# A linear-attention block followed by a three-way maxout layer: k and v laid out as five or four tokens per partition, projections in two-bank tiles, the maxima of q as a factor on the numerators, and a new order of the work

## The chip, the cores and the metric

One core of one Trainium2 chip. The time is device microseconds for one execution of the whole program. A core has TensorE (PE, with its weight loads PEld), VectorE (DVE), ScalarE (ACT), GpSimd (POOL) and SyncE (SP, here a queue for transfers), and 16 DMA engines that all queues share. [...]

## The reference

```
phi(x):  p = x @ w_phi                       # 64 -> 128 features
         p = p - max(|p|)                    # over the features, for each token
         concat(exp(p), exp(-p))             # 256 features
attention, for each of 8 batches x 8 heads, 576 tokens, 64 wide:
         kv = phi(k).T @ v ;  z = sum(phi(k))
         x  = (phi(q) @ kv) / (phi(q) @ z + 1e-6)
feed-forward, on 4608 tokens of 512 (the 8 heads side by side):
         h = max(x @ w1, x @ w2, x @ w3) ;  out = h @ w_out      # 512 -> 768 -> 512
```

Inputs and outputs are float32; products are made in bfloat16. Note that phi subtracts the maximum m *before* the sign is taken: the two halves are exp(p - m) and exp(-(p - m)), so m does not cancel between them.

## The kernel before, in words

**Units and chunks.** Attention is cut into 16 units (`attention`): four heads of one batch, two pairs of heads each. The feed-forward part is cut into nine chunks (`chunk`) of 512 tokens: one for each batch, for the first 512 tokens of it, and a last one for the 64 tokens left over in each of the 8 batches. A chunk needs both units of its batch.

**Layout.** A head's first 512 tokens lie four to a partition over 128 partitions; its last 64 tokens, the *tail*, lie one to a partition over 64 (L364-L376). So a unit has 18 tiles of 128 tokens: 16 main ones and two tail tiles, each made of the tails of two heads. One load brings a unit's main part, two more bring the tails of both units of a batch. For the first four units q and k are loaded by POOL with a cast to bfloat16 on the way (L472), apart from the first k, and turned on PE (L515, evicted at L518). From the fifth unit on they are loaded as float32 by SP, cast on POOL (L502), and turned by a DMA transpose, q and k side by side (L528).

**A unit, step by step.** *Projection* (L555): for each tile one product for q on the upper 64 rows and one for k on the lower 64 rows, each into a bank of its own for four tiles. *Exponentials of k*: `Ek`, both signs, from PSUM (L568). *Maxima*: DVE reduces the absolute values, `mk` and `mqp` (L574). *Factors of k*: `em` = exp(+-mk) is multiplied into v (`vab` L616, and `vtl` for the tails L631, both on POOL), so that Ek need not wait for the maxima. *Maxima of q*: in the first four units PE subtracts them with products of -1 (L655); from the fifth on PE turns the maxima (L582), ACT or DVE copies them out (L586), a DMA writes them as row 64 of `qkT` (L590), and a product with 65 rows (L651) gives p - m. *Exponentials of q*: `Eq`, from that product (L663). *K and N*: kv with z as a 65th column (L680, L683, evicted at L687), and the numerators with the denominator as a 65th column, both signs added in PSUM (L701). *Quotient*: reciprocal (L707) and product (L708) on DVE. *Turn of x*: on PE for the first six units (L721, evicted at L724), by a DMA transpose after that (L731).

**A chunk.** Two sets of six products `ups` (L754), with the weights w2 - w1 and w3 - w1; the first is evicted with a maximum against 0 (L762 on ACT, L764 on DVE), the second with a maximum against that (L760). Then for each of four tiles of 128 tokens a straight part x @ (w1 @ w_out) (L782) and the part of h (L787), evicted (L795) and stored (L802). The weights arrive by casting loads on POOL (L432); their differences are made on POOL and DVE (L829); w1 @ w_out is made on PE (L841, L855, L859).

**What sets the order.** A table in the source, `PLAN`, made by a planner, names for each node its engine, its start in the plan and the PSUM bank or buffer that it takes. `plan` reads it, `fill` puts small idle products on PE into gaps of the first 28 us. The engines are in-order queues; the framework puts the waits. `GATES` (L483) holds back some early loads of v until q and k of an earlier unit are turned.

Of the kernel before, what the change touches and what calls it, by code (L numbers as in the profile page):

```python
# [19 lines left out]
P = 128  # L20
CT = DM // P
JT = DFF // P

SM = 512
ST = S - SM
HU = 4
UNITS = B * H // HU
UT = 18
MT = 16
GROUPS = [(0, 4), (4, 4), (8, 4), (12, 4), (16, 2)]  # L30
BATCHES = [(0, 8), (8, 8), (16, 2)]
EW = UT * P + D
XW = SM + P
BY_PE = 4
X_PE = 6
SUBT = 4
HALVES = 1
WARM = 28.0
SLOW = 4.6
JOIN = 2  # L40
MOVE = 5
VA_DVE = 1
QK = 3
OSB = 4
K0_SP = 1
GATES = (None, (0, 0), (1, 0), (2, 0))
V_ACT = 4

class Buf:


    def __init__(self, pool, make):
        self.pool, self.make = pool, make
        self.users, self.tile, self.index, self.left, self.free = [], None, None, 0, 0.0
        self.locked = 0.0

    def __call__(self):
        if self.tile is None:
            self.tile = self.make(self)
        return self.tile  # L60


class Lock:
    locked = 0.0


class Slots:


    def __init__(self, n):  # L70
        self.last = [None] * n


class Node:


    def __init__(self, kind, u, costs, fn, deps, bufs, locks=(), lat=0.0, pipe=0.0, hold=None, dmas=1,
                 packet=60.0, mode=0):
        self.kind, self.u = kind, u
        self.costs, self.fn, self.deps = costs, fn, list(deps)  # L80
        self.bufs, self.locks, self.lat, self.pipe = list(bufs), list(locks), lat, pipe
        self.hold, self.dmas, self.packet, self.mode = hold, dmas, packet, mode
        self.start = self.end = self.eng = None
        for b in self.bufs:
            b.users.append(self)

PLAN = """  # L90
9S0@0.4 6G0@0.4 2D0@0.4 3D@0.8 4S@1.0 7G@1.2 0G@2.1 11S@2.2 1G@2.8 8S0@2.8 91G1@3.3 10A@3.5 13S@4.1 90G@4.2 5D@4.4
18T1@4.4 170G2@5.0 19D0@5.1 12A@5.3 15S0@5.3 168G@5.8 24T002300@5.9 92D@5.9 29T45@6.1 27D@6.4 25A@6.4 20T6@6.4
1143G@6.7 30A@6.8 28D@7.0 16G@7.5 21D@7.6 26A@7.8 17G@7.8 95G@8.1 32D@8.2 22T7@8.2 31A@8.2 94G@8.3 34T12@8.4 244G0@8.6
169S0@8.7 100T6@8.8 23D@8.8 35A@8.9 39T34@9.0 37D@9.1 44T7@9.3 243G@9.4 41A@9.5 42D@9.7 36A@10.0 171S0@10.0 47D@10.3
1146G@10.3 40A@10.4 33D@10.6 62T10@10.8 45A@10.9 1144G@11.1 59T3@11.2 14S@11.2 38D@11.2 49A0@11.4 63A@11.6 68T5@11.6
101D1@11.8 1145G@11.9 43D@12.0 46A@12.1 98T2@12.2 69A@12.4 96T6@12.6 48D@12.6 60A@12.9 247G@12.9 99D@13.0
122T11411@13.2 175G@13.2 61A@13.6 97D@13.6 117T72@13.8 93S@13.9 70A@14.0 65T3@14.2 125D@14.2 53A@14.5 121D@14.6
176G@14.8 64A@14.8 248G@15.0 177T6@15.1 120D@15.2 57G0@15.2 118A@15.3 179T5@15.5 126D@15.8 66A@15.8 107T17@16.1
178D2@16.1 124A@16.3 58G@16.5 67A@16.6 111D@16.7 181T6@16.9 123A@17.1 180D@17.3 119A@17.5 102T34@17.6 109A@18.0
182D@18.0 112T25@18.1 110D@18.2 52A0@18.4 71T6@18.4 108A@18.6 55G@18.6 116D@18.8 388S0@18.9 253T1@18.9 103A@19.1  # L100
254D0@19.4 1153T7@19.5 131A1@19.6 54G@19.6 105D@19.6 72A@19.8 1155T1@20.1 114A@20.2 115D@20.2 50G@20.6 136A1@20.7
1157T3@20.7 106D@20.8 56A@20.9 113A@21.1 140T21@21.3 1154D0@21.4 104A@21.6 51G@21.6 76T50@21.7 73A@22.1 143T4@22.3
127A@22.4 1158D@22.6 135G@22.6 77A@22.7 74T6@22.8 1156A@23.1 149T7@23.4 82T50@23.6 316S0@23.7 75D@23.7 128G1@23.9
137T3@23.9 151A@24.0 83D0@24.2 78T1@24.4 150A@24.5 80T6@24.7 172D1@24.8 142A@24.9 132G@24.9 79D1@24.9 251T5@25.1
144A@25.3 249T7@25.6 81D0@25.6 130A@25.8 129G@25.9 134A@26.0 146T1@26.1 141A@26.1 250D@26.3 84T6@26.5 318S@26.6
139A@26.6 201T00200@26.9 245D@26.9 133G@26.9 252D@27.0 152T71@27.1 145A@27.1 138A@27.6 85D1@27.6 86T4@27.7 154T5@28.1
153A@28.1 87D@28.3 202A@28.5 315S@28.5 158T31@28.7 147A@28.8 205D@29.0 156T6@29.0 1159T7@29.3 203A@29.4 157D0@29.6
155A@29.8 148A@30.2 159D1@30.2 88T4@30.6 204D@30.8 1160A@30.9 192T5610@31.0 162T3@31.6 200D@31.7 194A@31.7 1163T2@31.9
317S@32.3 199D@32.4 198A@32.5 195D@33.0 193A@33.0 160T7@33.2 197A@33.5 164T1@33.5 163D0@33.6 1165T5@33.8 165A@34.1
161D1@34.2 1148G@34.2 1164A@34.7 89D@34.8 273T11011@35.1 196D@35.3 183T3172@35.5 276D@35.9 166T4@36.0 184A@36.2  # L110
1149G@36.3 1161T6@36.3 167D@36.6 1166A@36.7 186D@37.1 174S@37.1 189A@37.2 1175T4@37.6 185A@37.7 190D@37.7 188A@38.1
1162D@38.3 392G1@38.4 218T50@38.5 275A@38.6 1147G@38.6 1179T3@38.9 1176A1@39.0 277D@39.1 187D@39.5 219A@39.5
1177T7@39.8 173S@40.0 191D@40.1 220A@40.1 274A@40.6 1150D@40.7 255T6415@40.8 1178A@40.9 1151D@41.3 215T2@41.3
260A@41.5 1169T0@41.8 322G2@41.8 1180D@41.9 257A@42.0 217A@42.5 1152D@42.5 1173T3@42.7 393G@42.9 261A@43.0 262D@43.1
321G@43.2 1185T7@43.5 258D@43.7 1174A@43.8 387S@43.8 206A0@44.3 391G@44.3 259D@44.3 1171T1@44.4 216A@44.5 1170D@44.9
256A@45.1 1183T3@45.3 210G0@45.3 263D@45.5 1186D@46.1 1181T6@46.1 264T2045@47.1 1182D@47.3 320S0@47.5 212T7@47.7
269A@47.8 267D@47.9 1189T6@48.1 213A@48.4 207G0@48.5 1172D@48.5 265A@48.8 1191T2@49.0 246S@49.0 272D@49.1 266A@49.5
271D@49.7 323S1@49.7 1201T1@49.8 211A@50.0 270A@50.2 1190D@50.3 208G@50.4 224T4@50.7 1184D@50.9 221T5@50.9 226A@51.2
1187T6@51.4 268D@51.5 223A@51.6 214A@52.1 1192D@52.2 209G@52.2 296T31@52.2 1197T0@52.5 390G@52.5 225A@52.6 1188D@52.8
278A1@52.9 298A@53.2 287T7@53.3 281G1@53.5 297A@53.7 284T2@53.8 283G1@53.8 222A@54.0 229T40@54.2 279G@54.4 290T3@54.8  # L120
230A@55.1 227T5@55.3 285A@55.5 237T40@55.9 289A@56.0 1198T@56.2 282G@56.3 292A@56.5 460S0@57.0 291A@57.1 1202T@57.5
280G@57.5 288A@57.6 461S@57.6 1199D0@57.8 286A@58.1 228D@58.4 238D0@58.8 342T00600@58.8 389S@58.9 233T3@59.0
1203A1@59.1 231T7@59.4 346D@59.4 458S0@59.5 234D1@59.7 324T0254@59.8 343A@59.9 528S@60.1 293T1@60.3 344A@60.4
331D@60.5 326A@60.7 299T31@60.8 327D@61.1 459S@61.3 325A@61.3 301T5@61.4 232D0@61.7 294A@61.8 1205T0@62.0 300A@62.3
332D@62.3 302A@62.7 394S2@62.8 235T7@62.9 328D@62.9 295A@63.1 305T31@63.2 307T5@63.5 345D@63.5 329A@63.6 309T2@63.8
308D1@64.1 303T1@64.2 330A@64.2 1206T@64.5 236D0@64.7 304D1@65.3 239T6@65.8 310D0@66.0 1207A2@66.0 333T5471@66.2
532G0@66.5 306D1@66.6 533G@66.7 313T2@66.8 335A@66.9 464G2@67.0 241T0@67.1 340D@67.2 1193T3@67.4 339A@67.4 336D@67.8
240A@67.9 531G@68.1 311T7@68.3 314D@68.4 338A@68.5 1194T@68.6 337D@68.9 242A@69.0 319S@69.1 465G@69.1 312D@69.5
334A@69.7 527S@69.7 413T11511@69.9 341D@70.0 395T6207@70.2 414A@70.3 1195D3@70.6 350A0@70.7 347T4@70.7 1215T1@70.8
401A@71.0 398D@71.2 348A0@71.5 1211T3@71.7 400A@71.7 417D@71.8 349S@71.9 402D@72.1 397A@72.2 1219T4@72.5 466S0@72.6  # L130
1216A0@72.7 403D@72.7 351G0@72.9 1212A@73.2 399D@73.3 1209T6@73.4 1220A@73.7 416D@74.0 404T0173@74.4 415A@74.4
355A0@74.8 352G@74.8 362T40@74.9 1210A@75.0 407D@75.1 1213T5@75.2 406A@75.5 412D@75.7 1223T6@76.0 364A@76.0 411D@76.3
1214A@76.5 354G@76.7 1217T0@76.9 597S0@76.9 353A@77.0 1224D@77.2 396A@77.2 665S@77.5 410A@77.7 408D@77.8 359T7@77.8
530G@77.9 418T5@78.0 371T20@78.1 363A@78.2 1218D@78.4 421A1@78.6 373T6@78.7 361A@78.9 419D1@79.0 423G1@79.0 596S0@79.1
368T4@79.3 1221T0@79.4 374D@79.6 370A@79.7 409A@80.0 485T00500@80.3 420S@80.3 372A@80.5 1229T6@80.5 488D@80.8
595S@81.0 1222D@81.1 486A@81.3 356T3@81.4 369A@81.6 1227T2@81.6 1204S@81.6 489D@81.7 405A@81.9 668G1@82.0 1230D@82.1
598S@82.2 487A@82.4 1225T0@82.5 1228D@82.7 358A@82.8 422G@83.0 365T4@83.3 357A@83.4 1208S@83.5 1226D@83.6
476T1652@83.7 360A@83.9 664S@84.1 433T31@84.2 367A@84.4 479D@84.4 430T0@84.4 1231T7@84.7 482A@84.9 601G2@84.9
# [130 lines left out]
def fill(order, spare, make, ready):  # L269
# [649 lines left out]
```

## Time and profile before

| | us |
|---|---|
| runs of the kernel before | 298.52, 300.09, 303.92 (median 300.09) |
| span of the profiled execution, first to last instruction | 298.8 |
| PE busy | 284.6 (95%) |
| DVE busy | 209.1 (70%) |
| ACT busy | 200.4 (67%) |
| POOL busy | 137.6 (46%) |
| moved by DMA | 50.02 MB in 87879 packets |

The profiled execution is known by its span alone; it lies between the fastest and the median run. In a row of a *table of groups* stand line, engine, operation, out<-in, shapes, count, then busy us and mean ns of one, then the idle time before and what ended it. A row of the *timeline* has start, length, engine, line, operation, tensors and how many neighbours were merged (x6). A row of the *chain* has start, length and what was being done on the way that ended last. A busy PE is not PE at its peak, because matmuls overlap; the distance between starts is the better measure.

### The profile page before, as it was taken

To read this page: it belongs to the slowest core of one execution; us is meant where nothing else is said; L and a number is where in the kernel's file an instruction comes from. 1 tells how busy PE (TensorE), PEld (TensorE's weight loads), DVE (VectorE), ACT (ScalarE), POOL (GpSimd) and SP (SyncE) were. 2 spreads that over 40 slices of the span, in tenths; PEclk is the share of its full clock that TensorE was granted. 3 is DMA by queue.
4 is the path that set the end of the run, shared out by engine and by line. 5 is a ranking of instruction groups with operands and counts; after the bars stand their busy time and mean duration, and the time that the engine had idled before them with its cause. 6 is when DMAs were issued, how large, how long until landed. Compare 5 with 4: busy or idle time off the path is not lost.

```text
span 298.8 us, 7548 instructions
## 1 busy us (share of the span) xinstructions
PE 284.6 (95%) x3002; PEld 162.8 (54%) x3002; DVE 209.1 (70%) x444; ACT 200.4 (67%) x463; POOL 137.6 (46%) x175
## 2 busy tenths in 40 slices
PE   7796899999999979999999999999999999999994
PEld 3464764467555636465555465546654475444452
DVE  4587689949979868879888678877887276315310
ACT  2587779686899869899877788478866870042111
POOL 8346875766277552593628482468070700000000
PEclk9989999999999999999999999999999999999998
DMA  7999999785097799959995839997434004320036
GB/s 152 188 201 246 237 245 239 210 216 165 0 234 234 137 233 268 276 149 221 242 325 138 160 114 259 253 233 220 78 85 115 36 3 77 114 110 2 0 125 156
DMA packets 87879, 50.02 MB, mean 167 GB/s; under 512 B 56100, under 2 KB 83364, under 8 KB 87844
## 3 DMA queue, kind: packets, MB, share of 16 engines
q1 hardware_dynamic: 81684, 44.50, 58.8%
q0 software_dynamic: 6080, 4.98, 10.5%
q8 instruction: 23, 0.38, 0.5%
q14 instruction: 12, 0.10, 0.1%
q10 hardware_dynamic: 80, 0.07, 0.1%
HBM read 34.67 MB, written 9.44 MB: 148 GB/s over the span
## 4 chain that ended last, share of the span: by engine, by line
PE 78%; DMA 13%; DVE 4%; SPq 1%; issue 1%; POOL 1%; POOLq 0%; DVEq 0%
PE ups L754 29%; PE ops L787 15%; PE ops L782 10%; PE psn L701 6%; DMA v_raw<-in_v_dram 5%; PE psq L555 5%; PE kvps L680 4%; PE psm L651 4%; DMA qkT<-qk_bf 3%; DMA k_raw<-in_k_dram 2%; DMA qkT<-mT 2%; PE pm L855 1%; DVE mk L574 1%; PE pxT L721 1%; PE kvps L683 1%
## 5 line engine op out<-in xcount | busy, mean ns | idle before, releaser
L754 PE MATMUL ups<-xT,w_bf 128*128 128x512 bf16 x432 | 102.5, 379 | 0.4 <-DVE hT L764 0.4
L663 ACT ACTIVATE Eq<-psm 128x512 bf16<-128x512 f32 (+1 forms) x160 | 82.6, 576 | 10.0 <-PE psm L651 8.0
L568 ACT ACTIVATE Ek<-psk 128x512 bf16<-128x512 f32 x128 | 72.4, 608 | 17.8 <-PE psk L555 12.8
L616 POOL TENSOR_TENSOR vab<-v_raw,em 128x1024 bf16<-128x1024 f32 (+1 forms) x36 | 61.1, 1714 | 41.1 <-ACT em L611 20.2
L754 PEld LDWEIGHTS <-w_bf 128*128 128x128 bf16 x432 | 40.5, 98 | 43.6 <-issue 0.6
L574 DVE TENSOR_REDUCE mqp<-psq 128x4 bf16<-128x512 f32 (+1 forms) x80 | 48.9, 630 | 9.0 <-PE psk L555 5.0
L787 PE MATMUL ops<-wout_bf,hT 128*128 128x512 bf16 (+1 forms) x222 | 51.2, 373 | 0.0
L760 DVE TENSOR_TENSOR hT<-hT,ups 128x512 bf16<-128x512 bf16 x54 | 35.8, 682 | 21.4 <-PE ups L754 12.0
L574 DVE TENSOR_REDUCE mk<-psk 128x4 f32<-128x512 f32 x64 | 42.9, 683 | 2.2 <-PE psk L555 1.2
L762 ACT ACTIVATE hT<-ups 128x512 bf16<-128x512 f32 x37 | 21.5, 602 | 32.3 <-PE ups L754 32.0
L787 PEld LDWEIGHTS <-hT 128*128 128x128 bf16 x222 | 21.2, 98 | 22.3
L708 DVE TENSOR_TENSOR x_sb<-psn,rden 128x320 bf16<-128x320 f32 x64 | 31.5, 492 | 2.2
L795 DVE COPY osb<-ops 128x512 f32<-128x512 f32 (+1 forms) x17 | 11.4, 673 | 26.4 <-PE ops L787 23.8
L701 PEld LDWEIGHTS <-Eq 128*128 128x128 bf16 x640 | 24.9, 98 | 6.5
L701 PE MATMUL psn<-kv_sb,Eq 128*128 128x65 bf16 x640 | 26.9, 194 | 0.0
L680 PE MATMUL kvps<-vab,Ek 128*128 128x65 bf16 x512 | 23.2, 194 | 2.2 <-POOL vab L616 2.2
L680 PEld LDWEIGHTS <-Ek 128*128 128x128 bf16 x512 | 21.7, 98 | 5.5 <-issue 2.3
L782 PE MATMUL ops<-xT 128*128 128x512 bf16 x96 | 24.5, 379 | 0.0
L502 POOL CAST qk_bf<-k_raw 128x128 bf16<-128x128 f32 (+2 forms) x22 | 15.7, 729 | 17.8 <-DMA k_raw<-in_k_dram 16.8
L795 ACT COPY osb<-ops 128x512 f32<-128x512 f32 (+1 forms) x20 | 11.6, 588 | 17.2 <-PE ops L787 16.9
L631 POOL TENSOR_TENSOR vtl<-v_raw,em 64x256 bf16<-64x256 f32 x32 | 19.6, 612 | 6.6 <-ACT em L611 3.7
L502 POOL CAST qk_bf<-q_raw 128x128 bf16<-128x128 f32 (+2 forms) x22 | 15.8, 728 | 14.9 <-DMA q_raw<-in_q_dram 8.7
(79 smaller groups left out, 332.2 us busy)
## 6 DMA issues: line engine op xcount, KB each, us to landing
v_raw<-in_v_dram SPq DMA_DIRECT2D x16, 512.0 KB, 6.2
out_dram<-osb SPq DMA_DIRECT2D x32, 256.0 KB, 2.7
k_raw<-in_k_dram SPq DMA_DIRECT2D x12, 512.0 KB, 5.8
q_raw<-in_q_dram SPq DMA_DIRECT2D x12, 512.0 KB, 4.7
w_bf<-in_moe_w_dram POOLq DMA_DIRECT2D x3, 768.0 KB, 22.2
q_raw<-in_q_dram SPq DMA_DIRECT2D x16, 64.0 KB, 9.8
k_raw<-in_k_dram SPq DMA_DIRECT2D x16, 64.0 KB, 5.1
v_raw<-in_v_dram SPq DMA_DIRECT2D x16, 64.0 KB, 6.3
```

The costliest lines, as they stand in the source:

```text
L502: copy_on[n_.eng](dst, raw_part(u, c, t0, t1))
L568: nc.scalar.activation(Ek[s]()[:, t0:t0 + n, :], of(1), EXP, scale=1.0 - 2.0 * s)
L574: nc.vector.tensor_reduce((mq, mk)[c]()[:, t0:t0 + n], of(c), AXX, ALU.max, apply_absolute_value=True)
L616: (nc.vector if n_.eng == "DVE" else nc.gpsimd).tensor_tensor(vab()[:, g, t0:t1, 0:D], raw_part(u, 2, t0, t1), em()[:, g, t0:t1].unsqueeze ...
L663: nc.scalar.activation(Eqb()[s][:, cols], psm()[:, 0:n * P], EXP, scale=1.0 - 2.0 * s)
L680: nc.tensor.matmul(kvps()[:, ab, g, :], lhsT=Ek[g]()[:, t, :], rhs=vab()[:, g, t, :], start=(g + ab + c == 0), stop=False)
L701: nc.tensor.matmul(psn()[:, c, :], lhsT=Eqb()[g][:, t0:t0 + P], rhs=kv()[:, pr, ab, g, :], start=(g == 0), stop=(g == 1))
L708: nc.vector.tensor_tensor(x_sb()[:, pr, :, ab, :], psn()[:, :, 0:D], rden().to_broadcast([P, 5, D]), ALU.mult)
L754: nc.tensor.matmul(ups(), lhsT=w_bf[i + 1][:, ct, j * P:(j + 1) * P], rhs=tokens_of(ct), start=(ct == 0), stop=(ct == CT - 1))
L760: nc.vector.tensor_tensor(hT()[:, j, :], hT()[:, j, :], ups(), ALU.max)
L782: nc.tensor.matmul(ops_()[:, 0:width], lhsT=tile_of(ct, tt), rhs=line_w[c_i > MOVE][:, ct, cols], start=(ct == 0), stop=False)
L787: nc.tensor.matmul(ops_()[:, 0:width], lhsT=hT()[:, j, tt * P:(tt + 1) * P], rhs=wout_bf[:, j, cols], start=False, stop=(j == JT - 1))
```

## The change

**Layout.** For k and v a head's 576 tokens now lie over 64 partitions per half: one half holds five tokens to a partition, the other four, and the second head of a pair the other way round, so that both heads of a pair fill nine tiles exactly and the tail tile (number 4) is shared. q keeps four tokens to a partition and a tail. One node loads q, k or v for a whole batch (for half of one at the very start) in four transfers, all on SP and all float32; POOL (and twice ACT and DVE) casts. q and k have buffers of their own, with the two pairs of a unit on the lower and the upper 64 rows.

**Loads.** The order is q, k of unit 0, k, q of unit 1, v of both. The weights are loaded by POOL after casts of unit 1. Three *gates*, one-element copies on POOL, hold k, q and v of batch 1 until the second, third and third set of weights has landed.

**Two-bank tiles.** PSUM is one tensor of eight banks; a tile may take two neighbours. Projections of q and of k are made for four tiles of both pairs, in pairs of 64-row products whose outputs lie in the two banks; reduces and exponentials take 1024 columns at a time.

**Maxima of q.** exp(p) and exp(-p) of q are taken without the maxima; the product that feeds them (M) has 64 rows, in pairs, 256 columns each. The two signs' numerators are kept apart in the two banks of a tile, and DVE adds them with the factor exp(-2m) on the first (the common factor exp(m) cancels in the quotient, but for the 1e-6, which the kernel before leaves out too). The quotient itself is a product in SBUF and may go to POOL.

**Others.** x is turned on PE for four units instead of six. Chunks 0 and 8 are split into halves of 256 tokens, so that the first half can start earlier; the very last output tile is split 384 + 128. `line_w`, `x_last` and four rotating `xT` have memory of their own. The order table is new, without times; small idle products (256 columns, 91 of them) are written into it.

```diff
+W_AFTER = ((1, "k"), (1, "q"), (1, "q"), (1, "q"))
+GATES = (("k", 1), ("q", 2), ("v", 2))
...
+    def pieces_kv(src, b, h0, n, dst):
+        heads = src[b, h0:h0 + 2 * n].rearrange("(r a) s d -> a r s d", a=2)
+        for a in range(2):
+            for hi in range(2):
+                c = 5 if a == hi else 4
+                s0 = hi * (5 - a) * HALF
+                t = 0 if a == 0 else (TAIL if hi else TAIL + 1)
+                yield (dst[hi * HALF:(hi + 1) * HALF, :, t:t + c, :].rearrange("p r c d -> p r (c d)"),
+                       heads[a, :, s0:s0 + c * HALF, :].rearrange("r (p c) d -> p r (c d)", p=HALF))
...
+            def gate(e, i=i, dst=dst):
+                nc.gpsimd.tensor_copy(dst()[0:1, 0, 0, 0:1], (w_bf + [wout_bf])[i][0:1, 0, 0:1])
...
-                        for c, ps in enumerate((psq, psk)):
-                            r = slice(c * D, (c + 1) * D)
-                            nc.tensor.matmul(ps()[:, i, :], lhsT=cols[r, :], rhs=w2[r, c, :], start=True, stop=True)
+                for r in range(2):
+                    rows = slice(r * D, (r + 1) * D)
+                    nc.tensor.matmul(two()[:, r * BANK + i * DF:r * BANK + (i + 1) * DF], lhsT=T()[rows, t, :],
+                                     rhs=w2[rows, r, :], start=True, stop=True)
...
-                    nc.tensor.matmul(psm()[:, 0:n * P], lhsT=wphi_m, rhs=qkT()[:, cols], start=True, stop=True)
+                        nc.tensor.matmul(two()[:, r * BANK + a * 2 * P:r * BANK + (a + 1) * 2 * P], lhsT=w2[rows, r, :],
+                                         rhs=Ts["q"]()[rows, t:t + 2, :].rearrange("p t c -> p (t c)"), start=True, stop=True)
...
+                nc.scalar.activation(e2()[:, :, :, 2 * h:2 * h + 2], m()[:, 0].rearrange("p r (a x) -> p r a x", a=2)[:, :, :, 2 * h:2 * h + 2],
+                                     EXP, scale=-2.0)
...
-                            nc.tensor.matmul(psn()[:, c, :], lhsT=Eqb()[g][:, t0:t0 + P],
-                                             rhs=kv()[:, pr, ab, g, :], start=(g == 0), stop=(g == 1))
+                                nc.tensor.matmul(to[:, a, c, :], lhsT=Eq[g]()[:, r, t0:t0 + P], rhs=kv()[:, r, a, g, :],
+                                                 start=True, stop=True)
...
-                    nc.vector.reciprocal(rden(), psn()[:, :, D:W])
-                    nc.vector.tensor_tensor(x_sb()[:, pr, :, ab, :], psn()[:, :, 0:D], rden().to_broadcast([P, 5, D]),
-                                            ALU.mult)
+                def y1(e, h=h, n=n, r=r, two=two, y=y):
+                    nc.vector.tensor_tensor(y()[:, :, 0:n, :], part(n, two, 0),
+                                            e2()[:, r, :, 2 * h:2 * h + n].unsqueeze(3).to_broadcast([P, 2, n, W]), ALU.mult)
+                def y2(e, n=n, two=two, y=y, rec=rec):
+                    nc.vector.tensor_tensor(y()[:, :, 0:n, :], y()[:, :, 0:n, :], part(n, two, 1), ALU.add)
+                    nc.vector.reciprocal(rec()[:, :, 0:n, :], y()[:, :, 0:n, D:W])
+                def quot(e, h=h, n=n, r=r, y=y, rec=rec):
+                    engines[e].tensor_tensor(x_sb()[:, r, 2 * h:2 * h + n, :, :].rearrange("p c a d -> p a c d"), y()[:, :, 0:n, 0:D],
+                                             rec()[:, :, 0:n, :].to_broadcast([P, 2, n, D]), ALU.mult)
...
+SPLIT = (0, 8)
+        halves = 2 if c_i in SPLIT else 1
```

In the new table a word such as `184P1` is node 184, on PE (P; D, A, G and S are DVE, ACT, POOL and SP), with the buffers or banks that it takes; `i7` is an idle product into bank 7. Node kinds of a chunk: `up`, `st`, `down` are the products of a chunk, `relu`, `max` and `osb` their evictions.

More of the change, by code (lines that the diff above doesn't have):

```diff
@@ L20 @@
 P = 128
+W = D + 1
 CT = DM // P
@@ L57, in __call__ @@
     def __call__(self):
         if self.tile is None:
-            self.tile = self.make(self)
+            self.tile = self.make(self.index)
         return self.tile
[L63 to L71, printed above, removed]
-class Node:
[L77 to L85, printed above, removed]
@@ L251, in plan, with __init__ @@
-def plan(nodes):
-    order = []
-    for word in PLAN.split():
-        what, start = word.split("@")
-        at = next(i for i, c in enumerate(what) if c.isalpha())
-        n, slots = nodes[int(what[:at])], iter(what[at + 1:])
-        n.eng, n.start = {"T": "PE", "D": "DVE", "A": "ACT", "G": "POOL", "S": "SP"}[what[at]], float(start)
-        n.end = n.start + n.costs[n.eng] + LATENCY[n.eng]
+class Node:
+    def __init__(self, kind, u, engines, fn, deps, bufs, locks, size, dmas):
+        self.kind, self.u, self.engines, self.fn = kind, u, engines, fn
+        self.deps, self.bufs, self.locks = list(deps), list(bufs), list(locks)
+        self.size, self.dmas = size, dmas
+        self.issued = False
@@ L293 @@
+        n.fn(word[at])
+        n.issued = True
+    assert all(n.issued for n in nodes)
 @with_exitstack
@@ L882 @@
-    order = plan(nodes)
-    def product(i):
-        def fn():
-            idler = psum.tile([P, SM], FP32, name="idler", tag=f"b{i}")
-            nc.tensor.matmul(idler, lhsT=idle, rhs=idle.unsqueeze(1).to_broadcast([P, 4, P]), start=True, stop=True)
-        return fn
-    for fn in fill(order, spare, product, n_idle.end):
-        fn()
+        rows = out[b * S:b * S + SM, :].rearrange("(p c) n -> p c n", c=4)
+        ready = [done[2 * b][h] + done[2 * b + 1][h] for h in range(2)]
+        chunk(b, ready, lambda ct, cols, b=b: xTs[b]()[:, ct, cols], [xTs[b]], lambda tt, rows=rows: [(rows[:, tt, :], slice(0, P))])
```

1075 lines of the change are left out of this document (434 added, 641 removed).

## The prediction, made before the result was known

> **What bounds the kernel now.** I read the totals of the page first, then the table of 30 us windows, then the chain that ended last, and only then single rows.
>
> ```profile
> span 298.8 us, 7548 instructions
> PE 284.6 (95%) x3002; PEld 162.8 (54%) x3002; DVE 209.1 (70%) x444; ACT 200.4 (67%) x463; POOL 137.6 (46%) x175
> 30.00:60.00 30.00, 28.81 (x366) 17.84 (x363) 25.49 (x54) 23.37 (x52) 22.61 (x22) 1.00 0.97 231
> 60.00:90.00 30.00, 30.00 (x390) 19.36 (x388) 22.88 (x51) 25.25 (x61) 17.14 (x19) 1.00 0.58 154
> 90.00:120.00 30.00, 27.88 (x355) 16.89 (x354) 24.90 (x57) 24.62 (x56) 15.62 (x22) 1.00 0.88 219
> 120.00:150.00 30.00, 30.00 (x342) 17.31 (x336) 24.66 (x53) 27.55 (x65) 19.67 (x24) 1.00 0.94 219
> 240.00:270.00 30.00, 30.00 (x263) 16.20 (x260) 14.53 (x33) 8.74 (x18) 0.40 (x1) 1.00 0.27 76
> ```
>
> The columns are PE, PEld, DVE, ACT, POOL, granted clock, DMA share and GB/s. From 30 us on PE has hardly a hole, at full clock; DVE stands at 0.76 to 0.85 of each window until 150 us and falls to a half only at the end. So PE sets the pace, and DVE is the next engine up. The chain shows the start, where it is otherwise:
>
> ```profile
> 5.13 7.38 DMA k_raw<-in_k_dram
> 16.75 16.24 DMA v_raw<-in_v_dram
> 34.14 2.06 POOL vab L616 x2
> 104.79 5.44 DMA qkT<-mT
> 256.73 7.77 PE ups L754 x36
> 265.36 10.36 PE ups L754 x48
> 294.83 0.42 DVE osb L795
> ```
>
> Until 33 us the chain is loads: v of the second unit lands 16.24 us after its issue. The first product of the feed-forward chunks (`ups`) starts at 46.37 us (timeline row below); from there to 294.8 us PE works nearly without pause, 248 us, and one loss inside is the maxima's way through memory (`qkT<-mT`, 5.44 us). Between 256.7 and 275.7 us there are only `ups`, 84 of 512 columns in 18.13 us, 0.216 us each.
>
> **PE, part by part.** PE matmuls overlap, so I use the distance between starts:
>
> ```profile
> 46.37 1.03 PE L754 MATMUL ups<-xT,w_bf 128*128 128x512 bf16 x4
> 92.29 0.38 PE L651 MATMUL psm<-qkT,wphi_m 128*128 128x512 bf16 x1
> 92.61 0.23 PE L555 MATMUL psq<-w,qkT 64*128 64x128 bf16 x1
> 93.00 0.22 PE L555 MATMUL psq<-w,qkT 64*128 64x128 bf16 x1
> 93.16 0.61 PE L651 MATMUL psm<-qkT,wphi_m 128*128 128x512 bf16 x2
> 95.33 1.10 PE L701 MATMUL psn<-kv_sb,Eq 128*128 128x65 bf16 x30
> L651 PE MATMUL psm<-qkT,wphi_m 128*128 128x512 bf16 x48 | 17.4, 380 | 2.1 <-DMA qkT<-mT 2.1
> L655 PE MATMUL psm<-minus,mqp 128*128 128x128 bf16 x72 | 7.5, 224 | 0.0
> ```
>
> Eight pairs of 64-row products start between 92.61 and 93.00 us, so a pair of 128 columns takes 0.055 us: both halves of the array work at once. Going into 64-row work costs 92.61 - 92.29 - 0.216 = 0.10 us, going out 93.16 - 93.00 - 0.055 = 0.10 us. A 65-column product takes (1.10 - 0.194) / 29 = 0.031 us.
>
> Removed: 64 full and 16 half `psm` (13.8 + 1.7 us), the 72 products that subtract the maxima in the first four units (4.0), 12 transposes of maxima (0.7), 640 numerator products (19.8), 144 half-width transposes at the start (about 4.7), 60 transposes of x (3.3): 48.0 us. Added: 64 pairs of 256 columns at 0.108 (6.9), 32 tail products at 0.055 (1.8), 512 numerator products of 65 and 64 of 130 columns (15.9 + 3.5), 72 full transposes (4.0), 40 of x (2.2): 34.3 us. The groups of 64-row work, counted as runs of neighbours in the order table, go from 48 (12 of them the half-width transposes) to 62; at 0.20 us each that adds 2.8 us. Net **-10.9 us** of PE work. A third (3.6 us) lies in units 0 and 1, before the first `ups`, where PE waits anyway. And before has, when `ups` begin, already turned q and k of units 2 and 3, projected unit 2 and finished the last product for `line_w`, some 5.5 us which the new table leaves for later (its gates hold batch 1 back). So PE work after the first `ups` falls by only 10.9 - 3.6 - 5.5 = **1.8 us**.
>
> **DVE.** Neighbours overlap here too:
>
> ```profile
> L574 DVE TENSOR_REDUCE mk<-psk 128x4 f32<-128x512 f32 x64 | 42.9, 683 | 2.2 <-PE psk L555 1.2 <-ACT Ek L568 0.9
> L708 DVE TENSOR_TENSOR x_sb<-psn,rden 128x320 bf16<-128x320 f32 x64 | 31.5, 492 | 2.2
> 125.52 1.28 DVE L574 TENSOR_REDUCE mqp<-psq 128x4 bf16<-128x512 f32 x2
> 128.64 0.17 DVE L707 RECIPROCAL rden<-psn 128x5 f32<-128x5 f32 x1
> 128.84 0.49 DVE L708 TENSOR_TENSOR x_sb<-psn,rden 128x320 bf16<-128x320 f32 x1
> 129.25 0.18 DVE L707 RECIPROCAL rden<-psn 128x5 f32<-128x5 f32 x1
> ```
>
> Two reduces of 512 take 1.28 us, so a step is 0.60 us. Between 320 columns (0.492) and 512 (0.683) a column costs 1.0 ns, leaving a fixed part of 0.16 us, of which 0.08 hides behind the next instruction unless that one needs the result. A reduce of 1024 is then a step of 0.60 + 0.53 = 1.13 us. Reduces per unit: before eight at 0.60 and two of 256 at 0.33, 5.5 us; after four at 1.13 and one at 0.60, 5.1: **-0.4 us a unit**. Merging two steps saves only the 0.08.
>
> The factor on the numerators is the costly part. Before, a quotient is 129.25 - 128.64 = 0.61 us, four a unit, 2.5 us. After, each of four groups has `y1` (numerator of one sign times factor), `y2` (plus the other sign) and the reciprocal, each needing the last: 260 columns 0.43 + 0.03, 390 columns 0.57 + 0.03, reciprocal 0.12. Per unit 4 x 0.46 + 4 x 0.60 + 4 x 0.12 = 4.7 us, and 14 of the 64 products with the reciprocal stay on DVE (0.4 a unit); the other 50 go to POOL. **+2.6 us a unit.** An operation of this form is not in the trace: it can't be below the 320-column row cut to 260 without a fixed part (0.27 us), nor above a 512-column one (0.68); over 128 of them that moves DVE by -33 to +19 us. I take the interpolation, close to the 320-column row.
>
> All told: 16 x 2.2 = 35 us more. The order table moves `relu` to DVE (17 to 29, 12 of them half-wide, +4), and evictions of `osb`, `kv`, x and transposes away (about -8). DVE goes from 209 to about **241 us**.
>
> **Where that bites.** From the first `ups` of chunk 0 to the first of chunk 4 I count in the new table for DVE 36 reduces of 1024 (40.7), 10 of 512 (6.0), 32 + 32 `y` (33.9) and 32 reciprocals (3.8), 18 full and 12 half maxima (14.8), 11 `relu` (5.3), 7 `osb` (4.2) and 24 small ones (about 10): 118 us. For PE: 60 `up`, 24 of them half-wide (41.5), 16 `st` and `down` (34.5), projections and factor-free exponent products (15), K and N (20), the rest and the switches (12): 123 us. A DVE share of 0.96 is needed where the four windows above show at most 0.85. Some stalls must come back; I put **+4 us**, from 0 (the planner's order hides all) to 15 (below).
>
> **ACT and POOL** have cover:
>
> ```profile
> L568 ACT ACTIVATE Ek<-psk 128x512 bf16<-128x512 f32 x128 | 72.4, 608 | 17.8 <-PE psk L555 12.8 <-DVE mk L574 4.0 <-DVE rden L707 0.6
> 124.48 3.28 ACT L568 ACTIVATE Ek<-psk 128x512 bf16<-128x512 f32 x6
> L616 POOL TENSOR_TENSOR vab<-v_raw,em 128x1024 bf16<-128x1024 f32 x28 | 53.0, 1905 | 39.2 <-ACT em L611 20.2 <-issue 9.8 <-DMA v_raw<-in_v_dram 8.0
> L631 POOL TENSOR_TENSOR vtl<-v_raw,em 64x256 bf16<-64x256 f32 x32 | 19.6, 612 | 6.6 <-ACT em L611 3.7
> L829 POOL TENSOR_TENSOR w_bf<-w_bf 128x1024 bf16<-128x1024 bf16 x3 | 6.3, 2129 | 1.2 <-DMA w_bf<-in_moe_w_dram 1.2
> ```
>
> Exponentials overlap by 0.608 - (3.28 - 0.608)/5 = 0.07 us, so halving 256 of them saves 128 x 0.07 = 9 us of ACT; 48 small factors (about 0.1 us each) and six more `kv` and six more `osb` evictions give 9 back: ACT stays near 200. POOL gains 50 quotients (0.61 to 0.83 us, from the 256-column row, +36), loses the tails' products (-20) and takes over casts: about 157 us, hidden with half the span to spare. The `mk` that `Ek` waits for (4.0 us) says that readers of one bank take turns; a two-bank tile is then held for 1.13 + 2 x 0.9 us, where a bank is held for about 1.8 now. Eight banks bear it on average (about half full by my count), so I price it at nothing, with the stalls of DVE as its upper bound.
>
> **The start.** All loads now go through SP's queue in the order q, k, k, q, v, and the weights start once k of unit 1 is cast. The rates of the first 60 us:
>
> ```profile
> q0 software_dynamic: 6080, 4.98, 52.4%
> q1 hardware_dynamic: 13760, 7.74, 52.3%
> ```
>
> Both queues took 31.4 us of all engines, 4.98 MB as written for the casting one, 7.74 MB for the other. The first chunk needs weights of 3.15 MB (19.9 us), batch 0 of 3.54 MB (14.4), and k of batch 1, released by the first gate, goes beside them (1.18 MB, 4.8): 39 us, plus 3 until data flows, so the last weight lands near **42 us**. The gates are new waits on POOL: the one for q of batch 1 waits for that last weight, and behind it in POOL's queue stand a cast (1.1 us), the last quotients of unit 1 (0.83) and the difference of weights (2.13) that the second kind of `ups` needs, near 46.5 us. The six half-wide `ups` of the first kind come before (2.6 us). So the chunks begin like a start at 43 instead of 46.4: **-3.5 us**, from -9 (all landed by 37) to +9. The end is a 128-column eviction for one of 256: -0.3.
>
> The rows above are of loads across 128 partitions; k and v now come in pieces of 64. [...] The pieces alternate between the halves, so two in flight could use all of the width.
>
> **The sum**, against the profiled execution: 298.8 - 3.5 (start) - 1.8 (PE work) - 0.3 (end) + 4 (DVE) = 297.2 us. The maxima's 5.44 us detour also goes, but its stall is small change against the new ones. The median of the runs, 300.09, lies 1.3 us above that span (lowest 298.52); I take half of it: **298 us**.
>
> **Rivals.** (a) *The start shrinks and DVE keeps up.* Weights and v land by 37 us, and the new order, free of the detour through memory, holds DVE at 0.96: 298.8 - 9 - 1.8 - 0.3 = 288 us. For it: ACT and PE already reach full windows, and the long `v_raw` wait of 16.24 us is mostly queueing. Against: no window shows such a DVE. (b) *DVE becomes the bound* between chunk 0 and chunk 4, the slower side. If it holds only 0.88 there, its 118 us take 134 where PE has 123: +11, so 298.8 - 5.6 + 11 = 304; at its present 0.83, 142 us, 312; I set 307. It decides below 0.92 (128 us, +5.6 cancels the gains). For it: the windows above; against: PE's work from other chunks can fill in. (c) *Half-wide loads*: if 64-partition pieces moved at half the 247 GB/s of q1's row, k and v of batch 0 (2.36 MB) would take 19.1 us instead of 9.6, and the start would move by +9.6 from 43 to 52.6: 298.8 + 6.1 - 2.1 + 4 = 307 us. Against it: the pieces' alternation. [...]
>
> **How the numbers follow.** The forecast has 0.42, (a) 0.30, (b) 0.20, (c) 0.08. Two per cent, about what a measurement of this kernel tells from no change, is 294.1 to 306.1. (a) falls below, (b) and (c) mostly above, the forecast within: faster 0.30, same 0.42, slower 0.28. The likeliest case alone reaches from 294 to 303; with the others the range is 287 to 311.
>
> **What would show it.** Right: DVE near 241 us and above 0.9 of the windows from 45 to 150 us; reduces of 1.2 us and `y` operations of 0.43 and 0.57; first `ups` between 40 and 45; PE's holes there released by DVE. Wrong: `ups` at 50 or later with PE waiting for weights or v (c); DVE holes as now and an end below 292 (a); long PE stalls on DVE (b); or PE pairs of 256 columns that start one after the other, which would take back 6.9 us.

## The result, and the profile after

The changed kernel takes 328.87 us (median of 4 runs, 325.59 to 330.42), the kernel before 299.82 in the same comparison: a ratio of **1.0961**, 95% interval 1.0893 to 1.1028. It is 29 us slower; the forecast was 298.0 and its range ended at 311. A time here is the median of all runs and a ratio compares fast runs alone, so the two need not agree to the last digit. First the totals of the page, its chain, two of its rows of queues, and the same windows as before:

```profile
span 326.7 us, 7715 instructions
PE 290.6 (89%) x3005; PEld 174.3 (53%) x3005; DVE 242.0 (74%) x439; ACT 201.4 (62%) x383; POOL 165.5 (51%) x180
q1 hardware_dynamic: 79744, 48.71, 67.9%
q0 software_dynamic: 2368, 3.15, 5.5%
PE 53%; DMA 17%; DVE 8%; SPq 7%; POOL 6%; issue 5%; ACT 2%; DVEq 0%; POOLq 0%
30.00:60.00 30.00, 28.10 (x336) 20.48 (x334) 26.99 (x57) 22.93 (x47) 21.10 (x21) 1.00 0.88 181
60.00:90.00 30.00, 22.55 (x303) 14.02 (x302) 25.04 (x45) 22.69 (x42) 19.18 (x17) 0.94 0.92 198
90.00:120.00 30.00, 27.06 (x285) 15.84 (x285) 20.82 (x39) 19.95 (x37) 17.12 (x20) 0.89 0.85 190
120.00:150.00 30.00, 28.29 (x310) 15.78 (x308) 24.39 (x42) 21.22 (x42) 20.03 (x21) 1.00 0.98 215
240.00:270.00 30.00, 29.38 (x290) 17.12 (x288) 25.13 (x48) 20.84 (x42) 12.40 (x15) 1.00 0.43 89
```

DVE has the work that was forecast (242.0 us against 241), but from 60 us on it is not saturated: 0.83, 0.69 and 0.81 of the windows. PE has the holes, 7.4 us in the window from 60, and loses clock there. So PE doesn't simply wait for a full DVE. From the first `ups` to the end the profile takes 284.7 us, before 252.4; PE's holes in that part are 23.6 us, before 3.1. The timeline shows the first `ups`, and a piece of the chain what PE waits for later:

```profile
41.98 0.60 PE L624 MATMUL ps<-xT,w_bf 128*128 128x256 bf16 x4 [0.42 <-DVE xT L228]
```

```profile
48.43 7.87 DMA k_raw<-in_k_dram
56.30 0.05 issue
56.35 1.15 POOL k_bf L228
57.52 1.40 SPq L360
...
60.84 5.69 DMA q_raw<-in_q_dram
...
68.15 1.15 POOL q_bf L228
69.32 3.36 DMA qT<-q_bf
72.68 0.05 issue
72.73 0.39 PE ps L407 x2
```

The start came out as forecast: the first `ups` begin at 41.98 us, before at 46.37. The loss is later. k of the third batch lands at 56.30 and its cast starts at 56.35; then SP issues the transposition and only behind it the load of q; the cast of q (68.15), its transposition (69.32) and PE (72.73) follow with at most 1.6 us between one and the next. Nothing here is an engine that is full: it is one line of transfers, casts and transfers. DMA time points the same way: the packets of q1 take 67.9% of the engines' span, before 58.8%, though in part because q1 now carries 48.71 MB instead of 44.50.

### The profile page after: what moved, and what is told of

The parts are those of the page before. It is cut to its first block, busy times and chain, and to the rows that moved or that the text cites. A ratio compares the mean times of both kernels' runs of the same rounds, so it can differ in the third digit from the quotient of the medians.

```text
span 326.7 us, 7715 instructions
## 1 busy us (share of the span) xinstructions
PE 290.6 (89%) x3005; PEld 174.3 (53%) x3005; DVE 242.0 (74%) x439; ACT 201.4 (62%) x383; POOL 165.5 (51%) x180
## 3 DMA queue, kind: packets, MB, share of 16 engines
q1 hardware_dynamic: 79744, 48.71, 67.9%
## 4 chain that ended last, share of the span: by engine, by line
PE 53%; DMA 17%; DVE 8%; SPq 7%; POOL 6%; issue 5%; ACT 2%; DVEq 0%; POOLq 0%
PE ps L624 21%; PE ps L651 9%; PE ps L646 7%; DMA qT<-q_bf 6%; DMA k_raw<-in_k_dram 6%; SPq L292 6%; PE ps L370 4%; PE ps L457 3%; DMA v_raw<-in_v_dram 3%; PE ps L517 3%; POOL k_bf L228 2%; POOL x_sb L539 2%; PE ps L477 2%; DMA q_raw<-in_q_dram 2%; DVE y L535 1%
## 5 line engine op out<-in xcount | busy, mean ns | idle before, releaser
L624 PE MATMUL ps<-xT,w_bf 128*128 128x512 bf16 (+1 forms) x432 | 95.5, 361 | 3.0 <-DVE hT L634 2.5
L433 POOL TENSOR_TENSOR vab<-v_raw,em 128x1152 bf16<-128x1152 f32 (+1 forms) x34 | 67.3, 1995 | 33.0 <-ACT em L426 12.0
L482 ACT ACTIVATE Eq<-ps 128x1024 bf16<-128x1024 f32 x64 | 63.3, 1029 | 11.9 <-PE ps L477 10.9
L385 ACT ACTIVATE Ek<-ps 128x1024 bf16<-128x1024 f32 x64 | 63.9, 1032 | 10.3 <-DVE m L380 6.2
L539 POOL TENSOR_TENSOR x_sb<-y,rec 128x256 bf16<-128x256 f32 (+1 forms) x50 | 35.7, 727 | 34.1 <-DVE rec L536 28.1
L651 PE MATMUL ps<-wout_bf,hT 128*128 128x512 bf16 (+2 forms) x222 | 51.6, 374 | 0.0
L398 DVE TENSOR_REDUCE m<-ps 128x8 f32<-128x1024 f32 x32 | 38.8, 1220 | 8.8 <-PE ps L370 8.4
L630 DVE TENSOR_TENSOR hT<-hT,ps 128x512 bf16<-128x512 bf16 (+1 forms) x66 | 37.7, 582 | 9.7 <-PE ps L624 5.5
L380 DVE TENSOR_REDUCE m<-ps 128x8 f32<-128x1024 f32 x32 | 38.6, 1216 | 2.4 <-PE ps L370 1.3
L646 PE MATMUL ps<-line_w,xT 128*128 128x512 bf16 x128 | 33.7, 388 | 2.4 <-DVE osb L228 1.1
L535 DVE TENSOR_TENSOR y<-y,ps 128x260 f32<-128x260 f32 (+1 forms) x64 | 31.4, 491 | 5.7 <-PE ps L651 0.5
L517 PEld LDWEIGHTS <-Eq 128*128 128x128 bf16 x512 | 24.7, 99 | 10.4 <-issue 2.6
L457 PEld LDWEIGHTS <-Ek 128*128 128x128 bf16 x512 | 23.3, 103 | 12.5 <-issue 8.7
```

What stands on the lines that cost most here:

```text
L380: nc.vector.tensor_reduce(m()[:, 1, :, t0:t0 + 4], two().rearrange("p (r c f) -> p r c f", r=2, f=DF), AXX, ALU.max, apply_absolute_value= ...
L385: nc.scalar.activation(Ek[g]()[:, :, t0:t0 + 4, :].rearrange("p r c f -> p r (c f)"), two().rearrange("p (r n) -> p r n", r=2), EXP, scale ...
L398: nc.vector.tensor_reduce(to, two().rearrange("p (r a c f) -> p r a c f", r=2, a=2, f=DF), AXX, ALU.max, apply_absolute_value=True)
L433: engines[e].tensor_tensor(vab()[:, g, p0 * UT:p1 * UT, 0:D], src_v()[:, r0 + p0:r0 + p1].rearrange("p r t d -> p (r t) d"), em()[:, g, p0 ...
L457: nc.tensor.matmul(to[:, a, g, :], lhsT=Ek[g]()[:, r, t, :], rhs=vab()[:, g, r * UT + t, :], start=(g + a + c == 0), stop=False)
L482: nc.scalar.activation(Eq[g]()[:, :, h * SM:(h + 1) * SM], two().rearrange("p (r n) -> p r n", r=2), EXP, scale=1.0 - 2.0 * g)
```

## The experiments

Ratios are to the kernel before, run on the same chip in the same comparison; one point (0.01) is 3.0 us. L numbers of experiments shift by a few lines.

**Which part costs.** Four edits of the changed kernel: stores issued by ACT; the loads left out; k and v loaded like q; the factor left out.

```diff
+        e = "A" if n.kind == "store" else word[at]
...
+            if b >= LEFT[what]:
+                return
...
-            for to, from_ in (pieces_q(b, 2 * r0, n, dst) if what == "q" else pieces_kv({"k": k, "v": v}[what], b, 2 * r0, n, dst)):
+            for to, from_ in pieces_q({"q": q, "k": k, "v": v}[what], b, 2 * r0, n, dst):
...
-                    nc.vector.tensor_tensor(y()[:, :, 0:n, :], y()[:, :, 0:n, :], part(n, two, 1), ALU.add)
+                    nc.vector.tensor_copy(y()[:, :, 0:n, :], part(n, two, 0))
```

> Three theories for the 328.9 us. L: the q, k and v loads and the DMA transposes come late, because they stand in SP's queue behind stores that wait for their evictions (63.2 us of SP waits). D: DVE, now 242 us, is the bound. H: the loads move slowly because k and v go in pieces of 64 partitions. Here every store is issued from ScalarE's queue, the order table otherwise unchanged. L: 308 to 322, about 315. D and H: 325 to 331, no change.

> Leaves out the loads of q and k from the third batch on and of v from the fourth on (the units work on the old data again); everything else as in the changed kernel. L and H: the holes go, 300 to 308. D: 322 or more, since DVE's work is unchanged.

> Undoes the layout of k and v alone: they are loaded as q is, four consecutive tokens per partition over 128 partitions and the rest as rows of one token; still four issues a load. H: 314 to 320. L and D: 326 to 332, no change.

> Leaves out the factor of q's maxima: both signs are summed in PSUM, the multiply (y1) is gone and the add (y2) is a copy, so DVE has 64 operations and about 31 us less; the same products on PE. D: 312 or less. L and H: 322 or more.

Measured: stores on ACT 334.84 us (1.1175, 1.1109 to 1.1241), slower; without loads 309.65 (1.0301, 1.0210 to 1.0392); k and v like q **313.46** (1.0496, 1.0427 to 1.0564); without the factor 322.79 (1.0787, 1.0726 to 1.0849). The third undoes only where a token lies and how its bytes come in, with the same bytes, casts and products, and gives back 4.65 points, 14 us. That is just beyond the 314 to 320 named for theory H, so H holds. D holds for a small part: 31 us of operations less on DVE (its busy time falls from 242.0 to 217.7) give 1.7 points. For L, taking the stores out of SP's queue brought nothing; whether ACT, which now issues them, lost what SP gained, this run can't say. The run without loads is just above the 300 to 308 named for it: the loads from the third or fourth batch on are worth 6.6 points. The page of the run with k and v like q, with two windows of it and two pieces of its chain:

```profile
PE 287.3 (92%) x3005; PEld 173.3 (56%) x3005; DVE 243.3 (78%) x439; ACT 200.9 (65%) x383; POOL 166.2 (53%) x180
q1 hardware_dynamic: 87936, 48.71, 63.4%
60.00:90.00 30.00, 25.39 (x337) 16.07 (x336) 27.35 (x48) 25.32 (x49) 21.68 (x22) 0.94 0.90 251
90.00:120.00 30.00, 29.88 (x309) 16.64 (x308) 25.12 (x47) 21.52 (x41) 18.60 (x21) 0.95 0.79 168
48.72 6.31 DMA k_raw<-in_k_dram
59.73 4.65 DMA q_raw<-in_q_dram
```

The same 48.71 MB, in more packets, now keep the engines busy for 0.634 x 310.9 = 197 us instead of 0.679 x 326.7 = 222. The piece of k on the chain takes 6.31 us instead of 7.87, and q, whose layout is the same in both, 4.65 instead of 5.69; why q gains too is not shown.

**Width, or number and size of the pieces?** On top of the layout of q, each large piece of k and v was cut in two, by partitions or by heads; beside them, before with half-wide loads, and layout and factor undone together.

```diff
+                cuts = [slice(0, HALF), slice(HALF, P)] if what != "q" and to.shape[0] == P else [slice(None)]
+                for c in cuts:
+                    engines[e].dma_start(to[c], from_[c])
...
+                cuts = [slice(0, n // 2), slice(n // 2, n)] if what != "q" and to.shape[0] == P else [slice(None)]
+                for c in cuts:
+                    engines[e].dma_start(to[:, c], from_[:, c])
...
-            eng.dma_start(dst[:, t0:t0 + MT, :].rearrange("p (h j) d -> p h (j d)", j=SM // P),
+            for rows in ((slice(0, D), slice(D, P)) if u >= BY_PE else (slice(0, P),)):
+                eng.dma_start(dst[rows, t0:t0 + MT, :].rearrange("p (h j) d -> p h (j d)", j=SM // P),
```

> The 128-partition layout of k and v of the third run (313.5 us), with its two large pieces of each load of k and v cut into partitions 0 to 63 and 64 to 127: six issues a load, the same bytes, now half-wide. H (a piece over 64 partitions is slow in itself): 322 to 332, most of the 15.4 us come back. I (the number of issues or the size of the pieces is what costs): the same as the run cut by heads within 3.

> As the run before it, but each large piece cut by heads: two pieces of half the bytes over all 128 partitions, six issues a load as well. H: 313 to 318, only the two more issues of 0.6 us. I: 322 to 332, the same as the run cut by partitions.

> The kernel before with one part of the change: the large loads of q, k and v of the units from the fifth on, and of v of the others where it goes by the same queue, are cut into partitions 0 to 63 and 64 to 127. If a half-wide load costs only where a load is what PE waits for, 298 to 304, since before has its loads early; if it costs by itself through contention, 308 or more.

> The layout of k and v undone and the factor of q's maxima left out together (that multiply is gone, 31 us less on DVE). If the two add up, 307.4 (313.5 less the 6.1 that leaving out the factor gave alone), 305 to 310. If DVE was hidden behind the late loads, 303 or less. If the loads were the cause of both, 311 to 314.

Measured: cut by partitions **337.19** us (1.1244, 1.1139 to 1.1349), cut by heads **323.96** (1.0819, 1.0740 to 1.0898). Six issues and the same bytes in both: the width alone is 4.2 points, 13 us. But I is not empty: both runs lie above what H named for them (322 to 332 and 313 to 318), and two more issues a load cost 3.2 points over the 313.46. The two pages' rows of q1 and of the large pieces (KB each, median us from issue to landing), by partitions first:

```profile
q1 hardware_dynamic: 88480, 48.71, 67.4%
v_raw<-in_v_dram SPq DMA_DIRECT2D x32, 256.0 KB, 6.4
k_raw<-in_k_dram SPq DMA_DIRECT2D x28, 256.0 KB, 5.2
```

```profile
q1 hardware_dynamic: 88480, 48.71, 61.5%
v_raw<-in_v_dram SPq DMA_DIRECT2D x32, 256.0 KB, 5.1
k_raw<-in_k_dram SPq DMA_DIRECT2D x28, 256.0 KB, 4.2
```

With equal packets and bytes the half-wide form takes 0.674 x 333.9 - 0.615 x 324.9 = 25 us more of the engines' time, and a piece lands 1.0 to 1.3 us later.

The profiles also show where the two more issues cost: at the start. In the run cut by heads v's last piece is issued at 16.06 us and lands 14.65 us later, and the first product with v waits for it; with four issues a load (first row) that product starts 8.8 us earlier:

```profile
22.05 1.73 POOL L433 TENSOR_TENSOR vab<-v_raw,em 128x576 bf16<-128x576 f32 x1 [4.63 <-DMA v_raw<-in_v_dram]
30.84 1.16 POOL L435 TENSOR_TENSOR vab<-v_raw,em 128x576 bf16<-128x576 f32 x1 [12.24 <-DMA v_raw<-in_v_dram]
```

The last load of weights stands behind it in POOL's queue, and the first `ups` move from 42.60 to 52.50 us; cut by partitions they begin at 50.91. From there on the run cut by heads takes 272.4 us against 268.3, in an execution whose granted clock, 0.916, was the lowest of its four. So most of the 3.2 points lies before the chunks, and the price of the width behind their start: from there on the run cut by partitions takes 283.0 us.

The kernel before with half-wide loads (only those from the fifth unit on were cut, no v of an earlier one) takes 307.66 us (1.0267, 1.0196 to 1.0337): between the two cases named for it, so even loads that PE hardly waited for cost something there (in the kernel before it waits 2.7 us for DMA after the first `ups`, none of it for a load). Layout and factor undone together give 305.28 (1.0184, 1.0118 to 1.0249): the two add up, as the first of the cases named ahead had it. The factor is worth 3.1 points here and 1.7 with the loads late; with intervals of 0.7 on each ratio these are hardly told apart.

**Is it only the order of the loads?** In the order table each load from the third batch on was moved up behind the last reader of its buffer; the same on the other two variants; and the kernel before with DVE's work doubled at the quotient. Of the order table the diff shows pieces of long lines.

```diff
-373G1 1069P2 162S 1053P0 1054D
+373G1 1069P2 162S 165S1 1053P0 1054D
...
-345A 390D1 165S1 336G
+390D1 336G
...
+                    for _ in range(2):
+                        nc.vector.tensor_tensor(x_sb()[:, pr, :, ab, :], psn()[:, :, 0:D], rden().to_broadcast([P, 5, D]),
+                                                ALU.mult)
```

> The changed kernel with nothing but the order of its loads altered: in the order table each q, k and v load from the third batch on stands right behind the last reader of its buffer (the cast, or the product with the factors), so that in SP's queue it passes up to 13 stores and transposes. S (the half-wide loads cost 15 us only because the order issues them 5 to 15 us after their buffer is free): 310 to 318. C (their price is contention or a rate that no order hides): 325 to 332.

> The same order of loads on top of k and v in q's layout (313.5 us). S: 307 to 311; the run without loads, 309.7, says that little more is to be had. C: 312 to 316.

> All three together: q's layout, early loads, and the factor of q's maxima left out (31 us less on DVE). If loads and DVE are all that the change costs apart from PE's switches, 298 to 303; if something else of the new order holds PE back, 304 to 307.

> The kernel before with each quotient multiplied twice (the second writes the same values): 64 more DVE operations of 0.49 us, 31 us, DVE from 209 to 240. If the kernel's order hides that much DVE work, 298 to 303; if DVE at 240 costs by itself what the run without the factor gave back, 305 to 309; if DVE becomes the bound, 310 or more.

All three with early loads got worse: 348.58 us (1.1623, 1.1535 to 1.1711), 336.79 (1.1216, 1.1119 to 1.1314) and 333.79 (1.1096, 1.0996 to 1.1196). My theory S fell, and C named no loss either. PE's longest waits, and SP's timeline around the hole of PE from 76.23 to 84.24 us, in the first of them:

```profile
PE ps L406 <- DMA qT<-q_bf: 22.1, 4, 8.9
PE ps L456 <- POOL vab L432: 5.0, 1, 5.0
```

```profile
70.67 2.59 SPq L291 DMA_DIRECT2D k_raw<-in_k_dram  x4
73.31 1.40 SPq L359 DMA_TRANSPOSE kT<-k_bf  x1
74.80 4.23 SPq L291 DMA_DIRECT2D q_raw<-in_q_dram  x4
79.19 4.12 SPq L359 DMA_TRANSPOSE qT<-q_bf  x2
```

q is cast by 72.8 us, but its transposition, which PE needs, now stands behind a transposition of k and a load for the next batch and is issued at 79.19: PE waits 22.1 us for `qT`, in the changed kernel 7.1. What is late is not the loads as such. Loads, transpositions and stores share SP's queue, and each place given to one is taken from another.

The doubled quotient in the kernel before takes **316.86** us (1.0594, 1.0533 to 1.0655): 18 us for 31 us of DVE operations (27.5 us of its busy time), the third of the cases named ahead. Its chain (the second line; the windows of before stand with the prediction) has 27% DVE:

```profile
PE 288.5 (91%) x2960; PEld 163.7 (52%) x3002; DVE 236.6 (75%) x508; ACT 200.8 (64%) x463; POOL 137.6 (44%) x175
PE 59%; DVE 27%; DMA 6%; issue 3%; SPq 1%; POOL 1%; ACT 1%; DVEq 0%; POOLq 0%
60.00:90.00 30.00, 26.89 (x323) 16.69 (x327) 23.07 (x51) 20.49 (x50) 13.87 (x16) 0.94 0.37 100
90.00:120.00 30.00, 28.46 (x351) 17.41 (x350) 27.18 (x59) 25.60 (x61) 18.43 (x25) 1.00 0.88 213
```

DVE is busy for 75% of the span there, in these windows for 0.77 and 0.91 of the time (before 0.76 and 0.83), and sets the end more often than its share says; the likely reason is that what follows waits for single results.

**What is left.** Loads and factor both left out; the control for before's half-wide loads; both costs in the old order; and `relu` moved from DVE to ACT.

```diff
-            eng.dma_start(dst[:, t0:t0 + MT, :].rearrange("p (h j) d -> p h (j d)", j=SM // P),
+            for hs in ((slice(0, HU // 2), slice(HU // 2, HU)) if u >= BY_PE else (slice(0, HU),)):
+                eng.dma_start(dst[:, t0:t0 + MT, :].rearrange("p (h j) d -> p h (j d)", j=SM // P)[:, hs],
...
+        e = "A" if n.kind == "relu" else word[at]
```

> Leaves out the loads of q and k from the third batch and of v from the fourth on, and the factor of q's maxima; k and v of the first batches in q's layout. If loads and DVE are the whole loss, 297 to 301; if the new order has a cost of its own (more changes between 64-row and full products, about 6 us in the traces), 302 to 306.

> Control for the kernel before with half-wide loads (307.7 us): the same large loads cut by heads, so as many issues, but over 128 partitions. If the width costs there, 299 to 303; if the issues and the smaller pieces cost, 306 to 309.

> The kernel before with both costs alone: half-wide loads (+7.4 us alone) and each quotient multiplied twice (31 us of DVE, +18.0 alone), in the old order. If they add, 325, which is nearly the changed kernel's 328.9; if one hides the other, 317 to 320.

> On top of q's layout for k and v (313.5 us): the 29 relu evictions that the new order table gives to DVE go to ScalarE (about 14 us less on DVE, as much more on ScalarE), nothing left out. If DVE's work sets the time at 0.2 us for each us, as the run without the factor says, 309 to 312; at 0.6, as the doubled quotients in the kernel before say, 303 to 307; if ScalarE's queue becomes the wait, 314 or more.

Measured: the floor **300.60** us (0.9978, 0.9921 to 1.0036); before cut by heads 299.18 (0.9997, 0.9951 to 1.0044); both costs in the old order 319.99 (1.0707, 1.0632 to 1.0782); `relu` on ACT 311.89 (1.0468, 1.0395 to 1.0540), in the first of its cases and not told apart from the 1.0496 without it. The page of the floor, then the last one's chain:

```profile
span 294.6 us, 7495 instructions
PE 280.1 (95%) x3005; PEld 169.3 (57%) x3005; DVE 218.9 (74%) x375; ACT 200.2 (68%) x383; POOL 165.6 (56%) x180
PE 78%; DVE 7%; ACT 6%; issue 3%; DMA 2%; POOL 2%; SPq 1%; DVEq 0%; ACTq 0%
```

```profile
PE 61%; DVE 15%; ACT 13%; issue 4%; DMA 4%; POOL 2%; DVEq 0%; ACTq 0%; POOLq 0%
```

Without those loads and the factor the new order stands where the old one does, with PE at 95%. So loads and factor make up the loss: of 9.6 points, 4.65 go to the half-wide layout, 3.1 more to the factor, and the last 2.1 to the loads that remain, as far as parts that overlap can be put in a row. The total hides a cost of the order itself, though:

| profile | span, us | first `ups` at | from there to the end |
|---|---|---|---|
| before | 298.8 | 46.37 | 252.4 |
| changed | 326.7 | 41.98 | 284.7 |
| k and v like q | 310.9 | 42.60 | 268.3 |
| that, without the factor | 302.7 | 39.84 | 262.9 |
| the floor | 294.6 | 36.96 | 257.6 |

The floor begins its chunks 9.4 us earlier than the kernel before and then takes 5.2 us longer; PE's changes of mode (below) are about half of that, and the rest is open.

In the old order the same loads cut by heads cost nothing, so width it is there too (2.7 points); the two costs together make 7.1 there (319.99, the case in which one hides the other), less than their sum of 8.6, and 2.5 short of the changed kernel. That DVE work moved to ACT bought nothing looks like a wait that changed its place: ACT has 13% of that chain, and 2% of the one without the move.

## Why the prediction was wrong

**The start: right.** First `ups` at 41.98 us, in the 40 to 45 that were named; the gain is 4.4 us where -3.5 stood. In three more profiles with the same loads up to there it lies between 40.62 and 43.77, so the size agrees only to a microsecond or two.

**PE's work: the size was off, with the wrong sign.** Summed from the distances between starts, as the prediction did, the useful work after the first `ups` falls by about 5 us (from some 239 to some 234), more than the forecast 1.8. But entering and leaving 64-row work, "62 runs for 48", was counted over the whole table. After the first `ups` the trace has 52 changes between 64-row and full products before and 104 after, and what they take beyond the products themselves goes from about 5 to about 12.5 us. So -1.8 is about +2 to +3. The pairs of 256 columns do run at once, as assumed: the two of a pair start 2 to 18 ns apart in 58 of the 64 pairs.

**DVE: work right, price too low.** The reduces, `y` and POOL's quotients have the forecast lengths:

```profile
L398 DVE TENSOR_REDUCE m<-ps 128x8 f32<-128x1024 f32 x32 | 38.8, 1220 | 8.8 <-PE ps L370 8.4 <-ACT osb L228 0.2
L531 DVE TENSOR_TENSOR y<-ps,e 128x390 f32<-128x390 f32 x32 | 17.7, 553 | 2.3 <-POOL x_sb L539 1.9
L535 DVE TENSOR_TENSOR y<-y,ps 128x260 f32<-128x260 f32 x32 | 13.6, 425 | 3.3 <-PE ps L651 0.5
L539 POOL TENSOR_TENSOR x_sb<-y,rec 128x256 bf16<-128x256 f32 x27 | 16.7, 623 | 22.8 <-DVE rec L536 17.0 <-issue 5.4
```

The +4 us for "some stalls must come back" measure as 5 (left out alone, 1.7 points) to 9 us (with the loads mended, 3.1 points). In the new order that is nearer to the forecast's +4 than to the +11 to +19 of rival (b); in the old order the doubled quotient cost 18, as (b) had it at DVE's present 0.83. So the price of DVE work depends on the order around it. The sign named for the forecast, DVE above 0.9 of the windows, failed with the late loads (0.83, 0.69, 0.81); with k and v like q one window reaches 27.35 of 30 us.

**The loads: the step that failed.** The sum had no term for q, k and v after the first chunk. Rival (c) priced half-wide loads, but only at the start, where they did little, and gave them 0.08. They cost 14 us, nearly all of it between 61 and 229 us (the same `ups` start 1.5 us earlier than with q's layout at the one end and 14.9 us later at the other), where k, q and v have one buffer each (v two) and a transposition or a cast waits for every load. Against (c) stood "the pieces alternate between the halves, so two in flight could use all of the width". That was reasoning without a row, and it did not hold: cut by partitions and cut by heads, with several pieces in flight at once (by partitions, six of k issued within 3.93 us at 115.66, a piece landing a median 5.2 us after its issue), differ by 13 us. Half of the 247 GB/s, in (c), was the author's assumption, and no run shows it; what the runs show is less: as an estimate, 24.7 us of engines' time more (222 less 197) over 18.9 MB of k and v, on 197 us for 48.71 MB, make a half-wide byte about a third dearer.

**POOL and SP: "hidden with half the span to spare" was the wrong question.** POOL has 165.5 us of work (157 forecast) and is half idle, but its casts stand in the chain between two transfers. **The two-bank tiles**, priced at nothing, can't hide a large cost either: the floor has them, and from its first `ups` on takes 5.2 us more than the kernel before, switches of PE included.

**Still open:** why v lands so much later at the start when it comes in six pieces (whether it falls behind the weights on the engines is not shown); in the old order no load of the start was cut, so its 299.18 says nothing on this. Nor was a new order made that places transpositions, loads and stores afresh. No variant beats the kernel before.

## What to carry to other kernels

Before you call a change of layout free, ask of every load that it touches how many partitions one transfer spans (here 64 instead of 128 cost 13 us, pieces being equal) and how long before its reader it lands; a load whose reader starts 0.05 us after it, as the cast of k here, has no cover. Count the waits of a queue and not only its work: SP, POOL and DVE were none of them full here (POOL busy for 51% of the span, DVE for 74%, and SP's stores alone waited 63.2 us for evictions), and each set the end somewhere (7%, 6% and 8% of the chain). Where a queue carries loads and transpositions, moving one up moves the other back: with the loads moved up PE waited 22.1 us for `qT` instead of 7.1.

## What the runs showed of the hardware that was not expected

Short holes cost PE its clock. Windows of the changed kernel, cut at the changes of the granted clock, with a hole in the first of each pair:

```profile
63.42:66.83 3.41, 1.04 (x32) 0.94 (x29) 1.69 (x3) 3.41 (x7) 3.24 (x4) 1.00 0.39 102
66.83:70.24 3.41, 3.41 (x41) 2.09 (x39) 2.38 (x4) 0.76 (x4) 3.41 (x4) 0.50 0.45 87
162.41:165.82 3.41, 1.45 (x12) 0.50 (x12) 3.37 (x5) 0.30 (x2) 1.66 (x3) 1.00 0.93 280
165.82:169.23 3.41, 3.41 (x16) 1.23 (x12) 2.41 (x3) 2.69 (x6) 2.96 (x3) 0.50 1.14 257
```

After a window of 3.41 us in which PE was busy for 1.04 or 1.45, the next 3.41 us run at half clock, though no hole in these two was longer than 2.4 us. In all, 20.5 us after the first `ups` ran at half clock, none in the kernel before until its end, so up to 10 us of the loss is the holes' echo. In the profiles of both kernels the changes of the granted clock lie whole numbers of 3.41 us apart (1 to 82). PE's busy time in such a window goes with what follows: with both profiles cut in these steps, each of the 6 full-clock windows with PE busy for less than 1.4 us was followed by half clock, and none of the 162 with more than 1.95 us; with all profiles but the one of lower clock the counts are 38 and 1369.
